# Queue order around xT, a later guard and later angle products in a gated-recurrence kernel with a cosine-gated feed-forward layer

## The chip, the core and the metric

The kernel runs on one core of one Trainium2 chip. The metric is the device time of one execution in microseconds (us). An engine takes its instructions strictly in the order of its own queue: TensorE (PE in the profile) multiplies, VectorE (DVE) and ScalarE (ACT) work elementwise, GpSimd (POOL) here does next to nothing but issue the DMAs of the guards, and SyncE (SP) issues all other DMAs. An instruction that waits holds up everything behind it in its queue.

## The reference

Two parts. The first is a linear recurrence with a complex decay for each of 4 batches and 8 heads, over 768 steps, with 48 x 48 states:

```python
mag = np.sqrt(a_re * a_re + a_im * a_im)
scale = np.minimum(mag, 0.999) / (mag + 1e-06)
a_re_n, a_im_n = (a_re * scale, a_im * scale)
for t in range(S):
    new_re = ar * S_re - ai * S_im      # ar, ai: the decay of step t
    new_im = ar * S_im + ai * S_re
    S_re, S_im = (new_re + kv, new_im)  # kv: k of step t times v of step t
    y[:, :, t] = np.einsum('bhd,bhde->bhe', q[:, :, t], S_re)
```

The second takes y, turned to x of 3072 tokens x 384, through a layer of width 2048:

```python
h = x @ w_in
g = h * np.cos(h)
return (g @ w_out).astype(np.float32)
```

## The kernel before

The sequence is cut into chunks of 128 steps. Two chunks make a group, so there are 12 groups, three to a batch. Within a chunk the recurrence becomes matrix products. Groups 0 and 1 and the conversion of the weights are written out by hand. After that, stage n of a loop (n = 2 to 11, lines 1730 to 1749) holds the work on several groups at once, and `weave` (line 1370) lays it out: each list of steps gets a stretch between 0 and 1, and the steps are traced in the order of their places. The order on each engine is then settled by a scheduler that goes through this trace with a clock of its own. A step that is earlier in the trace has priority, but a later one goes first where the earlier one isn't ready. `behind(a, b)` (line 543) fixes that a stands behind b in the queue that both use, without a wait. The order on PE is fixed by hand (`chain`).

What stage n holds, as far as it matters here:

- **Chunks of group n** (`chunks`, line 1417): the scores `sc` from kT and qT, the states `sp`, the outputs `yp`, which ACT copies to yT. Then `f_x` (line 1070) stores yT to DRAM as x, and `f_xt` (line 1079) loads it back turned, as xT. Then `ends` (line 844) sends one row of group n+1 out and back, and `load` fetches k, q and v of group n+2.
- **The first products of group n** (`first`, `mm1`, lines 1429 and 1230): `hp` from xT and w_in, at the end of the stage. ACT and DVE make the gates of them. In some of the eight, three short products take the place of one long one.
- **The second products of group n-1** (`seventh`, line 1314): seven products of quarters (Strassen's scheme) from gates and sums of gates. DVE forms those sums: `mixed` gives s1, `mixed_again` (line 1299) gives s3, then s2, then s4. In the trace an s2 mix reads `gate<-s,gate`. The third product reads the s2 mixes (`sum<-t_s,gate`). Results are stored from `ot` (lines 1350 and 1356).
- **The decay of group n+1**: `logs` (line 1409) runs `log_steps` (line 736), whose first step came at the end of the stage before. It ends in three products on DVE (lines 779, 785 and 788, the last of which reads im and writes tan) and a check of re on ACT (line 792). Then re and im of group n+2 are loaded into the same tiles, so these loads wait for the check and for the product with im. `prods` (line 1400) takes the sums over the steps (`lgs`), the arctangent of tan, the powers, and k and q times the powers. `phases` and `keys` (lines 1414 and 1383) go on with sine and cosine to `ks` and `qs`. DVE transposes these to `tr`, and `f_transpose` (line 945) sends tr out (`moved`) and loads kT in four pieces and qT in one. The next stage's scores read both.
- **A guard** (`guarded`, line 1443): GpSimd waits for a gate of group n-1, then loads 768 KB of raw weights into the buffer of tr, which ACT checks, and the same again. It waits for the gate tile with the highest number, 7. The order of the gates is 6, 7, 0, 1, 2, 3, 4, 5 in group 3 (4, 5, 0, 1, 2, 3, 6, 7 in group 2, plain from group 4 to 10).

k, q, re and im have one buffer each, and v has two. So k of group n+2 can be loaded once DVE has taken the product of k and the powers of group n+1.

Of the kernel before, what the change touches and what calls it, by code (L numbers as in the profile page):

```python
# [487 lines left out]
def fast_path(ctx, tc, q, k, v, a_re, a_im, moe_w_in, moe_w_out, out, least, odd, wide,  # L488
# [7 lines left out]
    nc = tc.nc  # L496
# [46 lines left out]
    def behind(ins, other):  # L543
        tc.add_manual_dep(ins.ins, other.ins.name, mybir.DependencyInfo(
            mybir.DependencyClass.NoSync, mybir.DependencyReason.DATA))
# [180 lines left out]
    def upper_half(g, x, scale):  # L726


        for name, tag in ("hi", "rs"), ("lo", "lo"):
            X[g][name] = gt.tile([C, G * DM], F32R, tag=tag, name=name)  # L730
        hi, lo = X[g]["hi"], X[g]["lo"]
        chain(nc.scalar.activation(out=hi, in_=x, func=AF.Copy, scale=scale))
        return lambda: vector.scalar_tensor_tensor(
            out=lo, in0=x, scalar=scale, in1=hi.bitcast(F32), op0=ALU.mult, op1=ALU.subtract)

    def log_steps(g, i, n):


        x = X[g]
        re, im = cut(x["re"], i, n), cut(x["im"], i, n)  # L740
        if i == 0:
            if g == 0:
                x["sin"] = temp("tan", 2)
            for name in "lg", "tan", "rs":
                x[name] = temp(name, 2 if name == "tan" else 1)
            both = gt.tile([C, 2, G * DM], F32, tag="pair", name="pair")
            x["Q"], x["mag"] = both[:, 0], both[:, 1]
        m2, sq, rs, mag = (cut(x[name], i, n) for name in ("lg", "tan", "rs", "mag"))
        for out_, in_ in (m2, re), (sq, im):
            if g == 0 and i > 0:  # L750
                if in_ is im:
                    yield
                vector.tensor_tensor(out=out_, in0=in_, in1=in_, op=ALU.mult)
            else:
                chain(nc.scalar.activation(out=out_, in_=in_, func=AF.Square))
        vector.tensor_tensor(out=m2, in0=m2, in1=sq, op=ALU.add)
        yield
        special(out=m2, in_=m2, func=AF.Ln, bias=tiny_b)
        special(out=mag, in_=m2, func=AF.Exp, scale=0.5)
        if g == 1:  # L760
            yield
        special(out=rs, in_=m2, func=AF.Exp, scale=-0.5)
        yield
        vector.scalar_tensor_tensor(out=mag, in0=re, scalar=0.0, in1=mag,
                                    op0=ALU.max, op1=ALU.add)
        vector.tensor_scalar(out=m2, in0=m2, scalar1=0.5, scalar2=math.log(CAP),
                             op0=ALU.mult, op1=ALU.min)
        yield
        special(out=rs, in_=rs, func=AF.Ln, scale=EPS, bias=one_b)
        special(out=sq, in_=mag, func=AF.Ln)  # L770
        special(out=sq, in_=sq, func=AF.Exp, scale=-1.0)
        yield
        vector.tensor_tensor(out=m2, in0=m2, in1=rs, op=ALU.subtract)
        yield

        lower = upper_half(g, m2, 1.0) if g >= PEG else None
        if lower and g > PEG:
            low = lower()
        product = vector.tensor_tensor(out=mag, in0=mag, in1=sq, op=ALU.mult)
        if lower and g > PEG:  # L780
            behind(product, low)
        elif lower:
            lower()
        yield
        vector.scalar_tensor_tensor(out=sq, in0=mag, scalar=2.0, in1=sq,
                                    op0=ALU.subtract, op1=ALU.mult)
        yield
        vector.scalar_tensor_tensor(out=sq, in0=sq, scalar=-1.0, in1=im,
                                    op0=ALU.mult, op1=ALU.mult)
        yield  # L790
        junk = stage["pool"].tile([C, DM], BF16, tag="below", name="below", bufs=1) if n == 1 else re
        checked = scalar.activation(out=junk, in_=re, func=AF.Relu, scale=-1.0,
                                    accum_out=odd[:, ds(next(odds), 1)])
        if g > PEG:
            behind(checked, tail["scalar"])

    def g_log(g, i, n):
        for _ in X[g].pop("steps", None) or log_steps(g, i, n):
            pass

    def summed_up(ps, g, i, name, ones):
# [497 lines left out]
    def mixed_again(g, p, name):  # L1299

        mix = X[g]["mix"][p]
        a, b = {"s3": ("s2", "s3"), "s2": ("s1", "s2"), "s4": ("s4", "s2")}[name]
        vector.tensor_tensor(out=mix[name], in0=mix[a], in1=mix[b], op=ALU.subtract)

    SEVEN = "a11", "a12", "a22", "s2", "s3", "s1", "s4"
    scale = 1.0 / (in_scale * out_scale)
# [7 lines left out]
    def seventh(g, p, part):  # L1314


        x, name = X[g], SEVEN[p]
        if p == 0 and part == 0:
            x["sum"] = pm.tile([C, E2], F32, tag="acc", name="sum", bufs=1)
            x["ot"] = [msb.tile([C, DM], F32, tag="ot", name="ot") for _ in range(G)]  # L1320

        alone = g == NG - 1 and p == 6
        summed = p in (0, 3, 5, 6) and not alone
        if not summed and part == 0:
            x["op"] = pm.tile([C, E2], F32, tag="m", name="op", bufs=2)
        ps = x["sum"] if summed else x["op"]
        for j in range(part * HJ // 2, (part + 1) * HJ // 2):
            matmul(ps, lhsT=left(g, name, j), rhs=right[name][:, j],
                   start=(j == 0 and (p == 0 or not summed)),
                   stop=(j == HJ - 1), skip_group_check=summed)  # L1330
        if part == 0:
            return
        c11, c12, c21, c22 = (x["ot"][i][:, ts(half, E2)] for i in range(2) for half in range(2))
        if g == NG - 1:
            c12 = rest
        if p in (0, 3, 5) or p == 6 and not alone:
            late["scalar"] = scalar.mul(out={0: c11, 3: c21, 5: c22, 6: c12}[p], in_=ps, mul=scale)
        if g == NG - 1 and p == 5:
            scalar.mul(out=c12, in_=ps, mul=scale)
        for part_ in {1: [c11], 2: [c21], 4: [c21, c22], 6: [c12] * alone}.get(p, []):  # L1340
            added = vector.scalar_tensor_tensor(out=part_, in0=ps, scalar=scale,
                                                in1=part_, op0=ALU.mult, op1=ALU.add)
            if alone:
                behind(added, late["read DVE"])
            late["vector"] = added
        row = g * G * C
        if g == NG - 1 and p == 1:
            behind(nc.sync.dma_start(out=out[ds(row, C), 0:E2], in_=c11), late["line"])
        elif p == 4:
            put = nc.sync.dma_start(out=out[ds(row + C, C), :], in_=x["ot"][1])  # L1350
            if g == NG - 1:
                behind(put, late["read SP"])
        elif p == 6 and alone:
            late["store"] = lambda: nc.scalar.dma_start(out=out[ds(row, C), E2:DM], in_=c12)
        elif p == 6:
            nc.sync.dma_start(out=out[ds(row, C), :], in_=x["ot"][0])

    def products(g, lo, hi):
        if g < PLAIN:
# [40 lines left out]
    def prods(g):  # L1400
        if not 0 <= g < NG:
            return
        if g not in (1, 2):
            yield from powers(g)
            yield lambda: g_angle(g, 0, G)
        yield lambda: (g_carry(g), g_split(g))
        yield lambda: (p_even(g, 0, G), p_apply(g, 0, G))

    def logs(g):
        yield from each(g_log, g)  # L1410
        if 0 <= g and g + 1 < NG:
            yield lambda: load(g + 1, ("re", "im"))

    def phases(g):
# [2 lines left out]
    def chunks(g):  # L1417
        for n in range(g * G, g * G + G):
            for hh in range(2):
                yield lambda n=n, hh=hh: f_scores(n, hh)  # L1420
            yield lambda n=n: f_state(n)
            yield lambda n=n: f_out(n)
        yield lambda: (f_x(g), f_xt(g))
        if PEG < g + 1 < NG:
            yield lambda: ends(g + 1)
        if g + 2 < NG:
            yield lambda: load(g + 2, ("k", "q", "v"))

    def first(g):
        late_ = [jp for jp in THREE if FROM[jp] == g + 1]  # L1430
# [8 lines left out]
    def wait_for(tile):  # L1439

        chain(nc.gpsimd.tensor_copy(out=after, in_=tile), "gpsimd")

    def guarded(g, count):

        if guards:
            yield lambda: wait_for(X[g]["gate"][NJ // 2 - 1][0:1, 0, 0:1])
        for _ in range(min(count, len(guards))):
            yield lambda: guard(guards.pop(0))

# [280 lines left out]
    for n in range(2, NG):  # L1730
# [4 lines left out]
        if FROM[THREE[0]] <= n < NG - 1:  # L1735
# [1 line left out]
        weave((mixes(n - 1, 2, 4), 0.0, 0.08), (logs(n + 1), 0.0, 0.02), (chunks(n), 0.0, 0.36),  # L1737
              (upper[2:] if plain else [], 0.0, 0.2), (products(n - 1, 0, 2 + (n < NG - 1)), 0.0, 0.365),
              (mixes_again(n - 1, "s3"), 0.06, 0.18), (mixes_again(n - 1, "s2"), 0.19, 0.27),
              (prods(n + 1), 0.2701, 0.2735), (second(n - 1, 1), 0.36, 0.5),  # L1740
              (mixes_again(n - 1, "s4"), 0.37, 0.48),
              (products(n - 1, 2 + (n < NG - 1), 7), 0.4, 0.56),
              (convert[0:1], 0.82, 0.82), (convert[1:2], 0.93, 0.93),
# [108 lines left out]
```

## Time and profile before

| | before |
|---|---|
| median of 3 runs | 653.19 us (650.83 to 653.82) |
| profiled execution | 651.08 us |
| its span, first to last instruction | 649.3 us |
| PE busy | 629.3 us (97%) |
| DVE busy | 522.2 us (80%) |
| ACT busy | 446.4 us (69%) |
| POOL busy | 30.8 us (5%) |
| granted TensorE clock | 0.999 |

A line of the timeline gives the start of a run of like instructions, its length, the engine, the line of the code, the operation, out<-in with shapes, and the count; in brackets stands the idle time ahead of it and what ended that. Line 691 is the helper through which nearly all matmuls go, line 680 that of most DVE and ACT instructions, line 711 that of ACT's table functions. SPq is the time that SyncE takes to issue a DMA, not the transfer. A line of the waits gives who waited for whom, the total in us, the number of waits and the longest. A line of the windows gives a stretch, its length, busy time of PE, PEld, DVE, ACT and POOL, the granted clock, the busy share of the DMA engines and what they moved in GB/s.

### The profile page before, as it was taken

The numbers are of one execution on the slowest core, as the hardware profiler recorded it, in microseconds if no ns is written. First come the engines' busy times: TensorE is split into PE (matmuls) and PEld (weight loads), VectorE is DVE, ScalarE is ACT, GpSimd is POOL, SyncE is SP. The second block draws the span as 40 slices with busy tenths as digits, with TensorE's granted clock in tenths as the row PEclk, the third lists the DMA queues.
The fourth block names the chain that finished last, engine by engine and source line by source line (L and its number), as shares of the span: only waits on it lengthen the run. The fifth ranks groups of instructions, "written<-read, shape, count | busy, mean of one in ns | idle before, by whom it ended". The sixth has DMA issues, their size and how long they took to land.

```text
span 649.3 us, 11364 instructions
## 1 busy us (share of the span) xinstructions
PE 629.3 (97%) x4279; PEld 571.5 (88%) x4279; DVE 522.2 (80%) x846; ACT 446.4 (69%) x803; POOL 30.8 (5%) x53
## 2 busy tenths in 40 slices
PE   8999999999998999999999999999999999999996
PEld 6888867777997889899999899899999899999996
DVE  6999989879789788798798888879878968964261
ACT  7898688284695697588588488589589479552340
POOL 4010200000000000000000000000000000000000
PEclk9999999999999999999999999999999999999999
DMA  9968755628538907927926935946945844351001
GB/s 240 246 184 207 223 167 124 171 49 225 116 89 189 258 2 175 224 91 177 249 63 143 248 97 123 245 98 162 235 94 144 232 87 124 132 111 49 24 1 32
DMA packets 232923, 94.94 MB, mean 146 GB/s; under 512 B 208701, under 2 KB 221246, under 8 KB 232858
## 3 DMA queue, kind: packets, MB, share of 16 engines
q1 hardware_dynamic: 225320, 68.51, 45.3%
q0 software_dynamic: 5824, 25.50, 12.1%
q8 instruction: 36, 0.59, 0.4%
q10 hardware_dynamic: 1714, 0.11, 0.2%
q14 instruction: 29, 0.24, 0.1%
HBM read 69.28 MB, written 24.81 MB: 145 GB/s over the span
## 4 chain that ended last, share of the span: by engine, by line
PE 69%; ACT 10%; DVE 8%; DMA 7%; issue 3%; SPq 1%; ACTq 0%; DVEq 0%
PE hp L691 29%; PE op L691 13%; PE sum L691 8%; PE sc L691 5%; PE yp L691 4%; DMA xT<-x 4%; PE sp L691 3%; PE hb L691 3%; DMA im<-in_a_im_dram 2%; DVE pair L680 2%; ACT tan L711 1%; DVE tan L680 1%; ACT rs L711 1%; PE phs L691 1%; SPq L584 1%
## 5 line engine op out<-in xcount | busy, mean ns | idle before, releaser
L691 PE MATMUL hp<-xT,w_in 128*128 128x256 f32 (+1 forms) x768 | 165.6, 373 | 5.9 <-DMA xT<-x 5.2
L691 PEld LDWEIGHTS hp<-xT,w_in 128*128 128x128 f32 x768 | 141.5, 190 | 27.2 <-DVE qs L680 4.4
L711 ACT ACTIVATE gate<-hp,half_pi_b 128x512 f32<-128x512 f32 x96 | 65.9, 687 | 72.1 <-PE hp L691 56.0
L691 PE MATMUL op<-w_out,gate 128*128 128x192 f32 (+1 forms) x464 | 102.7, 371 | 0.0
L691 PEld LDWEIGHTS op<-w_out,gate 128*128 128x128 f32 x464 | 78.7, 190 | 15.2 <-issue 0.4
L680 DVE TENSOR_TENSOR gate<-hp,gate 128x512 f32<-128x512 f32 x62 | 42.4, 686 | 30.7 <-ACT junk L680 30.3
L680 ACT ACTIVATE junk<-hp 128x512 bf16<-128x512 f32 x96 | 56.7, 590 | 0.0
L691 PE MATMUL sum<-w_out,gate 128*128 128x192 f32 x304 | 54.9, 328 | 0.4 <-DVE gate L680 0.4
L691 PE MATMUL sc<-qT,kT 96*128 96x128 f32 x384 | 51.0, 278 | 2.1 <-issue 1.8
L691 PEld LDWEIGHTS sc<-qT,kT 96*128 96x128 f32 x384 | 47.2, 191 | 5.1 <-issue 2.7
L691 PEld LDWEIGHTS sum<-w_out,gate 128*128 128x128 f32 x304 | 49.3, 190 | 0.8 <-DVE gate L680 0.7
L680 DVE SCALAR_TENSOR_TENSOR gate<-hp,gate 128x512 f32<-128x512 f32 x34 | 23.5, 691 | 22.8 <-ACT junk L680 22.8
L691 PE MATMUL hp<-xh,wh 128*128 128x256 f32 x204 | 36.9, 290 | 0.0
L680 DVE TENSOR_TENSOR atm<-sc,causal 128x512 f32<-128x512 f32 x48 | 32.5, 685 | 5.2 <-PE sc L691 5.0
L691 PE MATMUL hp<-xl,wl 128*128 128x256 f32 x204 | 35.2, 281 | 0.0
L680 ACT COPY yT<-yp 48x512 f32<-48x512 f32 x44 | 25.4, 578 | 13.8 <-PE yp L691 13.1
L680 DVE TENSOR_TENSOR gate<-gate 128x256 f32<-128x256 f32 x80 | 31.7, 418 | 3.1 <-PE op L691 2.5
L691 PE MATMUL yp<-atm,v 128*48 128x128 f32 x352 | 33.5, 277 | 0.0
L680 ACT ACTIVATE ot<-sum 128x192 f32<-128x192 f32 x39 | 12.5, 321 | 29.3 <-PE sum L691 29.3
L707 ACT ACT_TABLE_LOAD x24 | 30.8, 1283 | 1.2 <-PEq L1836 0.7
L691 PE MATMUL sum<-t_s,gate 128*128 128x192 f32 x160 | 29.4, 330 | 1.6 <-DVE gate L680 1.6
L691 PEld LDWEIGHTS hp<-xh,wh 128*128 128x128 f32 x204 | 29.8, 189 | 0.5
(163 smaller groups left out, 1246.2 us busy)
## 6 DMA issues: line engine op xcount, KB each, us to landing
moved<-tr SPq DMA_DIRECT2D x20, 768.0 KB
raw<-in_moe_w_in_dram POOLq DMA_DIRECT2D x16, 768.0 KB, 5.9
raw<-in_moe_w_out_dram POOLq DMA_DIRECT2D x16, 768.0 KB, 5.0
kT<-moved SPq DMA_DIRECT2D x40, 192.0 KB
qT<-moved SPq DMA_DIRECT2D x10, 768.0 KB
k<-in_k_dram SPq DMA_DIRECT2D x24, 192.0 KB
q<-in_q_dram SPq DMA_DIRECT2D x24, 192.0 KB
v<-in_v_dram SPq DMA_DIRECT2D x24, 192.0 KB
```

Source lines behind the costliest of these rows:

```text
L584: put(out=tile_[lo:hi, i_], in_=steps[lo + by:hi + by, i_])
L680: ins = getattr(self.engine, op)(**kw)
L691: chain(nc.tensor.matmul(out, **kw), "tensor")
L707: chain(nc.scalar.preload_act_table_set(table))
L711: chain(nc.scalar.activation(func=func, **kw))
```

## The change

Four edits:

1. `load` of k, q and v of group n+2 goes through `back_first`, which puts each of these DMAs behind the last DMA of xT in SyncE's queue. The two stores of `ot` are put behind it too.
2. The guard waits for the gate that is last in the order of its group.
3. `log_steps` yields "angles" ahead of the three products, for groups above 2. `g_log` stops there, and a new step `angles`, at 0.2695 to 0.2699 of the stage, goes on. The first of the three products is put behind the last s2 mix (`late["mixed"]`). The check of re on ACT is put behind what ACT's chain held last at the split of the logarithm (`late["upper"]`).
4. The loads of re and im of group n+2 move with the products, from the end of `logs` (by 0.02 of the stage) to the end of `angles`.

```diff
         lower = upper_half(g, m2, 1.0) if g >= PEG else None
+        late["upper"] = tail["scalar"]
         if lower and g > PEG:
-            low = lower()
+            lower()
+            yield "angles"
         product = vector.tensor_tensor(out=mag, in0=mag, in1=sq, op=ALU.mult)
-        if lower and g > PEG:
-            behind(product, low)
-        elif lower:
+        if "mixed" in late:
+            behind(product, late["mixed"])
+        if lower and g == PEG:
             lower()
...
         if g > PEG:
-            behind(checked, tail["scalar"])
+            behind(checked, late["upper"])
 
     def g_log(g, i, n):
-        for _ in X[g].pop("steps", None) or log_steps(g, i, n):
+        x = X[g]
+        x["steps"] = x.get("steps") or log_steps(g, i, n)
+        for at in x["steps"]:
+            if at == "angles":
+                return
+
+    def g_rest(g):
+        for _ in X[g]["steps"] if g > PEG else []:
             pass
...
-        vector.tensor_tensor(out=mix[name], in0=mix[a], in1=mix[b], op=ALU.subtract)
+        late["mixed"] = vector.tensor_tensor(out=mix[name], in0=mix[a], in1=mix[b], op=ALU.subtract)
...
             put = nc.sync.dma_start(out=out[ds(row + C, C), :], in_=x["ot"][1])
-            if g == NG - 1:
-                behind(put, late["read SP"])
+            behind(put, late["read SP"] if g == NG - 1 else late["x"])
...
         elif p == 6:
-            nc.sync.dma_start(out=out[ds(row, C), :], in_=x["ot"][0])
+            behind(nc.sync.dma_start(out=out[ds(row, C), :], in_=x["ot"][0]), late["x"])
...
     def logs(g):
         yield from each(g_log, g)
-        if 0 <= g and g + 1 < NG:
+
+    def angles(g):
+        if g < NG:
+            yield lambda: g_rest(g)
+        if g + 1 < NG:
             yield lambda: load(g + 1, ("re", "im"))
...
         if g + 2 < NG:
-            yield lambda: load(g + 2, ("k", "q", "v"))
+            yield lambda: load(g + 2, ("k", "q", "v"), put=back_first)
+
+    def back_first(**kw):
+        put = nc.sync.dma_start(**kw)
+        behind(put, late["x"])
+        return put
...
         if guards:
-            yield lambda: wait_for(X[g]["gate"][NJ // 2 - 1][0:1, 0, 0:1])
+            yield lambda: wait_for(X[g]["gate"][X[g]["order"][-1]][0:1, 0, 0:1])
...
-              (prods(n + 1), 0.2701, 0.2735), (second(n - 1, 1), 0.36, 0.5),
+              (angles(n + 1), 0.2695, 0.2699), (prods(n + 1), 0.2701, 0.2735), (second(n - 1, 1), 0.36, 0.5),
```

## The prediction

> **What bounds the kernel now.** I read the page first, then the waits of TensorE, then the timelines of PE, SP, DVE, ACT and POOL in stages 3 to 10, and last the chain of waits and windows of half a us.
>
> ```profile
> span 649.3 us, 11364 instructions
> ...
> PE 629.3 (97%) x4279; PEld 571.5 (88%) x4279; DVE 522.2 (80%) x846; ACT 446.4 (69%) x803; POOL 30.8 (5%) x53
> ```
>
> PE is busy for 97% of the span, so no faster engine can bring much: all that can be won is PE's idle time, some 20 us with the start and the tail. The profiled execution took 651.08 us, 2.11 below the median of 653.19 and inside the runs (650.83 to 653.82). I work the sum out against it and subtract the result from the median.
>
> ```profile
> PE hp L691 <- DMA xT<-x: 5.2, 5, 1.8
> PE sum L691 <- DVE gate L680: 2.0, 5, 0.5
> ```
>
> These two waits, 5.2 and 2.0 us, are idle time of PE that repeats in the loop. The timeline of PE shows where they fall, and a third one:
>
> ```profile
> 206.59 15.81 PE L691 MATMUL hp<-xT,w_in 128*128 128x256 f32 x72 [1.84 <-DMA xT<-x]
> ...
> 228.47 1.13 PE L691 MATMUL sc<-qT,kT 96*128 96x128 f32 x8 [1.81 <-issue]
> ...
> 260.52 1.75 PE L691 MATMUL hp<-xT,w_in 128*128 128x256 f32 x7 [0.54 <-DMA xT<-x]
> ...
> 279.58 1.13 PE L691 MATMUL sc<-qT,kT 96*128 96x128 f32 x8
> ...
> 359.84 10.60 PE L691 MATMUL hp<-xT,w_in 128*128 128x256 f32 x48 [1.34 <-DMA xT<-x]
> ...
> 378.83 1.06 PE L691 MATMUL sc<-qT,kT 96*128 96x128 f32 x8
> ...
> 396.46 2.22 PE L691 MATMUL sum<-t_s,gate 128*128 128x192 f32 x12 [0.37 <-DVE gate L680]
> ...
> 410.44 1.75 PE L691 MATMUL hp<-xT,w_in 128*128 128x256 f32 x7 [0.31 <-DMA xT<-x]
> ...
> 429.43 1.05 PE L691 MATMUL sc<-qT,kT 96*128 96x128 f32 x8
> ...
> 509.56 10.60 PE L691 MATMUL hp<-xT,w_in 128*128 128x256 f32 x48 [1.16 <-DMA xT<-x]
> ...
> 528.55 1.06 PE L691 MATMUL sc<-qT,kT 96*128 96x128 f32 x8
> ```
>
> The brackets at 206.59, 260.52, 359.84, 410.44 and 509.56 are the five waits of the first products for xT: 1.84, 0.54, 1.34, 0.31 and 1.16 in stages 3, 4, 6, 7 and 9. At 396.46 stands one of five waits for an s2 mix, 0.37; their mean is 2.0 / 5 = 0.4, and stages 4, 6, 7 and 9 have one each. At 228.47 the scores of stage 4 wait 1.81 us, put down to "issue". The other rows of scores show no idle time ahead; I use them below.
>
> **Edit 1, k, q, v and the stores behind xT.** SP's queue and DVE's in stage 7:
>
> ```profile
> 396.85 2.46 SPq L584 DMA_DIRECT2D im<-in_a_im_dram  x4
> 399.42 2.16 SPq L1075 DMA_DIRECT2D x<-yT  x2
> 405.01 1.02 SPq L584 DMA_DIRECT2D k<-in_k_dram  x2
> 406.14 0.67 SPq L1084 DMA_DIRECT2D xT<-x  x1
> ...
> 412.06 1.49 SPq L1350 DMA_DIRECT2D out_dram<-ot  x1
> ```
>
> ```profile
> 395.12 0.94 DVE L680 SCALAR_TENSOR_TENSOR tan<-tan,im 128x768 f32<-128x768 f32 x1
> 395.99 1.09 DVE L680 TENSOR_TENSOR gate<-s,gate 128x256 f32<-128x256 f32 x3
> ...
> 404.03 0.95 DVE L680 TENSOR_TENSOR pair<-k,pair 128x768 f32<-128x768 f32 x1
> ```
>
> The k load is issued at 405.01, when DVE's product of k and the power ends (404.03 + 0.95 = 404.98). xT stands right behind it and goes out at 406.14, though its own condition, that x has landed, can be met earlier. How much earlier, and what it costs to run with k's packets ahead:
>
> ```profile
> 299.94 1.72 SPq L1075 DMA_DIRECT2D x<-yT  x2
> ...
> 305.29 0.37 SPq L1084 DMA_DIRECT2D xT<-x  x1
> ...
> 550.67 0.38 SPq L1084 DMA_DIRECT2D xT<-x  x1
> ```
>
> ```profile
> 406.14 4.16 DMA xT<-x
> ```
>
> ```profile
> 553.00:553.50 0.50, 0.50 (x4) 0.50 (x4) 0.50 (x2) 0.31 (x1) 0.00 (x0) 1.00 0.48 164
> 553.50:554.00 0.50, 0.50 (x5) 0.50 (x4) 0.50 (x2) 0.48 (x2) 0.00 (x0) 1.00 0.00 0
> ```
>
> In stage 5 x is issued until 301.66 and xT goes out at 305.29, with SP idle just before, so x takes at most 3.6 us to land. In stage 7 it would be there at 401.58 + 3.6 = 405.2, 0.9 before 406.14. Behind k's 2 x 192 KB xT takes 4.16 us. In stage 10, where no k is loaded, it is issued at 550.67, and the traffic ends in the slice from 553.0 (0.48 busy, then none): about 2.8 us, and I take 3.0 with the signal. So xT should land at 408.2, 2.1 earlier than at 410.3, and that is more than any of the five waits. Bounds of this edit: nothing, up to 5.2. The stores stand behind xT already (412.06 after 406.14); that part removes nothing, and adds at most a wait that is met. What is queued behind the later k, q and v is the row of the decays and `moved`, which is the question further down.
>
> **Edit 3, the products behind the s2 mixes.** Nothing is added. In stage 7 three of the s2 mixes (1.09 us) run after the product with im. Put ahead of it, they end some 3 us earlier, as three products of 0.95 no longer stand before them, and the wait of 0.4 goes. The product with im then ends at 396.06 + 1.09 = 397.15. Its first reader is the arctangent:
>
> ```profile
> 398.75 0.84 ACT L711 ACTIVATE tan<-tan 128x768 f32<-128x768 f32 x1
> ```
>
> ACT gets to it at 398.75, after its exponentials and a table load, so 1.6 us of cover remain; without that cover each us would go into the keys. The im load waits for the same product and is later by 1.09; its next reader, the first step of a logarithm, stands behind the first products, which start 13 us after 396.85 (410.44). But x is issued behind im (399.42 after 396.85 + 2.46), so x may be up to 1.09 later too. Taken off the 2.1 this leaves 1.0, enough for stages 4 and 7, about enough for 9, and 0.3 short in stage 6 and 0.8 in stage 3. If the scheduler instead sends x out before im, which is now late, xT has over 3 us to spare. Either fits the result, as the next bound is elsewhere. The check of re keeps its length and its place behind the split.
>
> **Edit 4** moves ten DMA issues per stage with these products, and has no cost of its own.
>
> **Edit 2, the guard.** Kept for last, because it shows that next bound:
>
> ```profile
> 216.25 0.74 POOL L631 DMA_DIRECT2D raw<-in_moe_w_in_dram  x1 [0.58 <-ACT junk L680]
> ```
>
> ```profile
> 215.69 6.53 SPq L960 DMA_DIRECT2D kT<-moved  x4
> 222.33 0.78 SPq L962 DMA_DIRECT2D qT<-moved  x1
> ...
> 273.20 0.80 SPq L962 DMA_DIRECT2D qT<-moved  x1
> ...
> 367.05 3.91 SPq L960 DMA_DIRECT2D kT<-moved  x4
> 371.06 1.09 SPq L962 DMA_DIRECT2D qT<-moved  x1
> ...
> 422.02 1.22 SPq L962 DMA_DIRECT2D qT<-moved  x1
> ...
> 521.74 0.64 SPq L962 DMA_DIRECT2D qT<-moved  x1
> ...
> 566.96 5.15 SPq L960 DMA_DIRECT2D kT<-moved  x4
> ```
>
> In group 3 gate 7 is the second of eight. So the guard's 768 KB start at 216.25, in the middle of the four kT loads, whose issue then takes 6.53 us against 3.91 in stage 6. qT follows at 222.33, and the scores wait for it: 228.47 - 222.33 = 6.14 us. With the gate that is last, the load starts after the first products, and qT goes out about 2.6 earlier. The bounds are nothing (kT is slow for another reason) and both idle times of that stage, 1.81 + 1.84 = 3.65. I take 2.6. In all other groups gate 7 is last anyway.
>
> [...]
>
> **What is late next.** The same rows say how early the scores could start. Stage 5's follow qT's issue by 279.58 - 273.20 = 6.38 without a wait, so 6.14 to 6.38 is the landing, and I take 6.25. The room of the others, each for the first products ahead of it: stage 5 0.1; stage 7 378.83 - 371.06 - 6.25 = 1.5; stage 8 429.43 - 422.02 - 6.25 = 1.15; stage 10 528.55 - 521.74 - 6.25 = 0.55. qT depends on DVE's transposes, hence on the arctangent and on the scores of the stage before, and not on xT. So time won at xT or at the s2 mixes comes back as a wait for qT as soon as it exceeds the room.
>
> | stage | idle that goes | room | gain |
> |---|---|---|---|
> | 3 | 1.84 + 1.81 | 2.6 from the guard | 2.6 |
> | 4 | 0.54 + 0.4 | 0.1 | 0.1 |
> | 6 | 1.34 + 0.4 | 1.5 | 1.5 |
> | 7 | 0.31 + 0.4 | 1.15 | 0.7 |
> | 9 | 1.16 + 0.4 | 0.55 | 0.55 |
>
> The sum is 5.45: 651.08 becomes 645.6, and the median 653.19 - 5.45 = 647.7.
>
> **The rivals.**
>
> - *qT is no floor.* k, q and v are out sooner where xT is, `moved` starts on emptier DMA engines and qT lands earlier by what is needed. Then all idle time goes: 5.2 + 2.0 + 1.8 = 9.0, 644.2. Against it: qT's chain starts at the arctangent, which doesn't move.
> - *The bytes are only put off.* k, q and v, 1.15 MB, lie closer to `moved`, kT and qT on the same DMA engines, and qT lands later by the 1.1 us for which k stood ahead of xT. The rooms shrink by 1.1: stage 3 gives 1.5, 4 loses 1.0, 6 gives 0.4, 7 nothing, 9 loses 0.55. That is 0.35, so 652.8: no change. [...] Against it: in the last stage, with no k, q or v loaded, the issue of kT still takes 5.15 us (566.96), no less than with them.
> - *Slower.* The scheduler keeps the s2 mixes where they are and only the products go back. The last mix ends at 395.99 + 1.09 = 397.08, the three products at 397.08 + 3 x 0.95 = 399.9, and im, with x behind it, is late by 399.9 - 396.06 = 3.9. xT has 2.1 of that; the other 1.8 falls on the five stages with waits, 9.0, and the guard gives 2.6 back: 653.19 + 6.4 = 659.6. It decides from a delay of 2.1 + 2.6 / 5 = 2.6 on. Against it: no mix has anything else to wait for, and each has priority over the products in the new trace.
> - *It doesn't do what it says.* The orders are a scheduler's; the stores were behind xT before, and a changed trace may put something else there, such as the check of re between the exponentials (0.9 late in each arctangent, inside the cover). Then the guard alone is left: 653.19 - 2.6 = 650.6, or nothing.
>
> **How the numbers follow.** A measurement of this kernel can tell about 0.5%, 3.3 us, from no change. My forecast has 0.55, qT as no floor 0.13, the bytes put off 0.14, slower 0.08, and the change without its effect 0.10. Faster by more than 0.5% are the first two, less a little for a forecast whose guard term fails (2.85 left): 0.66. Slower by more than that is 0.08 and half of 0.02 for delays between; I say 0.09. The rest, 0.25, is the same. The range goes from the largest gain, 644.2, less 1.2 for runs as low as the profiled one, to the case of the bytes put off, a little short of it: 643.0 to 652.0. What lies outside is the slower case and part of the unchanged ones, about 0.15 to 0.2.
>
> **What would show it.** Right: in SP's timeline xT before k, and from it no idle time ahead of `hp`; no wait of `sum` for `gate`; the guard's load of stage 4 after its scores have begun, instead of at 216.25; kT's issue near 216 taking about 4 us; and small idle times ahead of the first scores of stages 5, 7 and 10, where now there are none. Wrong: the scores of those stages without idle time (then the gain is larger), x issued later than the end of `yp` by more than today with a wait for xT left (the slower case), or an arctangent later against the scores than 398.75 - 378.83 = 19.9 us.

## The result and the profile after

| | before | after |
|---|---|---|
| median | 653.51 us (650.83 to 654.52, 4 runs) | 670.61 us (669.76 to 671.38, 4 runs) |
| profiled execution | 651.08 us | 671.38 us |
| its span | 649.3 us | 669.6 us |
| granted clock | 0.999 | 0.984 |

The ratio is 1.0268, with a 95% interval of 1.0234 to 1.0302: slower, where the prediction said faster. By the medians that is 17.1 us; the two profiled executions differ by 20.3, as the one before, 651.08, lies near the fastest of its runs. The page's first lines, and the waits of TensorE after:

```profile
span 669.6 us, 11345 instructions
...
PE 632.7 (94%) x4279; PEld 574.6 (86%) x4279; DVE 522.5 (78%) x846; ACT 446.7 (67%) x803; POOL 29.8 (4%) x53
```

```profile
PE hp L691 <- DMA xT<-x: 20.5, 2, 10.6
PE yp L691 <- DVE atm L680: 2.0, 5, 0.9
PE sc L691 <- DMA qT<-moved: 1.6, 2, 0.8
PE sc L691 <- issue: 1.5, 1, 1.5
...
PE sum L691 <- DVE gate L680: 0.4, 1, 0.4
```

VectorE, ScalarE and GpSimd are as busy as before, within 1 us; PE is busy for 3.4 us more, at a lower clock (below). The five short waits for xT and the s2 waits are gone, as forecast (the 0.4 left stands in the tail, and stood there before: the prediction counted it among its five s2 waits). But two waits for xT have come that were not there, 20.5 us together; the span is longer by 669.6 - 649.3 = 20.3. The timeline of PE shows them in stages 2 and 3:

```profile
150.38 2.74 PE L691 MATMUL op<-w_out,gate 128*128 128x384 f32 x8
163.71 22.57 PE L691 MATMUL hp<-xT,w_in 128*128 128x256 f32 x96 [10.59 <-DMA xT<-x]
186.11 1.06 PE L691 MATMUL sc<-qT,kT 96*128 96x128 f32 x8
...
226.44 18.43 PE L691 MATMUL hp<-xT,w_in 128*128 128x256 f32 x72 [9.94 <-DMA xT<-x]
248.99 1.06 PE L691 MATMUL sc<-qT,kT 96*128 96x128 f32 x8
```

Before, the row of the first of these scores was:

```profile
174.36 1.06 PE L691 MATMUL sc<-qT,kT 96*128 96x128 f32 x8
```

The scores of stage 3 (the row of `sc` behind the first products of stage 2) start at 186.11 instead of 174.36, 11.75 late, and those of stage 4 at 248.99 instead of 228.47, another 8.77. From there to the end of the span it is 669.6 - 248.99 = 420.6 after and 649.3 - 228.47 = 420.8 before: nothing more is lost, and nothing gained. Why xT is late stands in SyncE's timeline of the same two stages, with VectorE's beside it:

```profile
145.04 1.69 SPq L1084 DMA_DIRECT2D x<-yT  x2
153.67 0.36 SPq L1269 DMA_DIRECT2D out_dram<-ot  x1
158.46 0.34 SPq L966 DMA_DIRECT2D moved<-tr  x1
158.97 0.37 SPq L1093 DMA_DIRECT2D xT<-x  x1
...
208.79 0.82 SPq L1084 DMA_DIRECT2D x<-yT  x2
221.08 0.34 SPq L966 DMA_DIRECT2D moved<-tr  x1
221.53 0.38 SPq L1093 DMA_DIRECT2D xT<-x  x1
...
423.47 0.39 SPq L1093 DMA_DIRECT2D xT<-x  x1
...
424.85 1.02 SPq L1442 DMA_DIRECT2D k<-in_k_dram  x2
```

```profile
156.25 2.19 DVE L680 STREAM_TRANSPOSE tr<-ks 128x1536 f32<-128x1536 f32 x1
...
218.87 2.19 DVE L680 STREAM_TRANSPOSE tr<-ks 128x1536 f32<-128x1536 f32 x1
```

Between x and xT stands `moved`, the transfer of the next group's keys. It waits for VectorE's transpose, which ends at 156.25 + 2.19 = 158.44 and 218.87 + 2.19 = 221.06, and it is issued 0.02 us later each time. xT, whose data had long landed (x is issued by 146.73 and 209.61, and the DMA share is 0.00 from 152.5 to 154.5 and from 215.5 to 221.5), goes out right behind it. In stage 2 a plain store stands there as well, until 153.67. From stage 4 on the queue is as intended: in stage 7 xT goes out at 423.47, and k behind it at 424.85.

### The profile page after: what moved, and what is told of

Read it like the earlier page. It is cut to its first block, busy times and chain, and to the rows that moved or that the text cites. A ratio compares the mean times of both kernels' runs of the same rounds, so it can differ in the third digit from the quotient of the medians.

```text
span 669.6 us, 11345 instructions
## 1 busy us (share of the span) xinstructions
PE 632.7 (94%) x4279; PEld 574.6 (86%) x4279; DVE 522.5 (78%) x846; ACT 446.7 (67%) x803; POOL 29.8 (4%) x53
## 4 chain that ended last, share of the span: by engine, by line
PE 65%; DVE 12%; ACT 11%; DMA 7%; issue 4%; SPq 1%; ACTq 0%; DVEq 0%
PE hp L691 23%; PE op L691 15%; PE sum L691 10%; PE sc L691 5%; PE yp L691 5%; PE sp L691 3%; DVE gate L680 2%; DMA qT<-moved 2%; DMA xT<-x 2%; ACT gate L711 2%; ACT junk L680 2%; DVE hp L680 1%; PE hb L691 1%; DVE pair L680 1%; PE phs L691 1%
## 5 line engine op out<-in xcount | busy, mean ns | idle before, releaser
L691 PE MATMUL hp<-xT,w_in 128*128 128x256 f32 (+1 forms) x768 | 170.1, 381 | 21.3 <-DMA xT<-x 20.5
L691 PEld LDWEIGHTS hp<-xT,w_in 128*128 128x128 f32 x768 | 144.5, 194 | 43.7 <-DMA xT<-x 21.4
L691 PE MATMUL sp<-v,ks 128*96 128x48 f32 x320 | 29.7, 246 | 0.0
```

The lines of the kernel that those rows point to most:

```text
L691: chain(nc.tensor.matmul(out, **kw), "tensor")
```

## Theories

**Q, the head of the queue.** Edit 1 pins k, q, v and the stores behind xT, but `moved` is pinned to nothing. With what stood around xT gone, the scheduler put `moved` ahead of xT in stages 2 and 3, and SyncE's queue stood still for its wait. **A rival, the angle edit:** im, and x behind it, go out later, and the products of VectorE stand elsewhere. **Another, the bytes:** k, q and v meet `moved`, kT and qT on the DMA engines. Q says that a pin that restores the order gives the forecast's time; the rivals say that it doesn't.

## The experiments

Each ratio is to the kernel before on the same chip (medians 649.69, 650.01 and 650.56 us in the three groups: e1 to e4, e5 to e8, e9 to e12). `late["x"]` is the last DMA of xT.

**The order mended.** The changed kernel, with `moved` and the last plain store behind xT:

```diff
-        nc.sync.dma_start(out=moved.rearrange("q (r b) x j -> (q r) b x j", b=NB), in_=tr)
+        behind(nc.sync.dma_start(out=moved.rearrange("q (r b) x j -> (q r) b x j", b=NB), in_=tr), late["x"])
...
+            if g == 1 and i:
+                behind(put, late["x"])
```

> The changed kernel with two more NoSync edges: the transposed keys and queries (moved) and the last plain store of group 1 stand behind xT in SyncE's queue. Theory Q (queue): in stages 2 and 3 xT stands behind the keys' moved in the queue and waits for DVE's transpose; both idle times of 10.6 and 9.9 us go, with the slow clock after them, and the time comes to 646 to 651 us. Rival A (angles): x or im is late because the angle products are late, and xT would wait anyway: the idle times stay, 665 us or more. Rival C (contention): x lands late, since its bytes share the DMA engines: the idle times shrink by less than half, about 660 us.

Measured: 645.37 us, ratio 0.9936 (0.9914 to 0.9958); and again in the third group:

> The same kernel as in the first of these runs (the changed kernel with the keys' transfer and the last plain store behind x), as the standard of the runs beside it on this chip. Expected at the ratio that it had: 0.9914 to 0.9958, 644 to 647 us. The interval decides what the guard and the angle edit are worth in the runs below.

Measured: 645.46 us, 0.9923 (0.9897 to 0.9950). The span of the profiled execution is 642.8 us. Its SyncE in stage 3, its PE in stages 2 and 3, and its waits:

```profile
196.68 0.82 SPq L1084 DMA_DIRECT2D x<-yT  x2
200.00 0.38 SPq L1093 DMA_DIRECT2D xT<-x  x1
...
208.88 2.46 SPq L966 DMA_DIRECT2D moved<-tr  x2
213.88 3.69 SPq L969 DMA_DIRECT2D kT<-moved  x4
```

```profile
153.11 7.93 PE L691 MATMUL hp<-xT,w_in 128*128 128x256 f32 x36
161.72 13.22 PE L691 MATMUL hp<-xT,w_in 128*128 128x256 f32 x60 [0.67 <-DVE gate L680]
174.77 1.06 PE L691 MATMUL sc<-qT,kT 96*128 96x128 f32 x8
...
204.37 16.04 PE L691 MATMUL hp<-xT,w_in 128*128 128x256 f32 x72
224.52 1.06 PE L691 MATMUL sc<-qT,kT 96*128 96x128 f32 x8
```

```profile
PE yp L691 <- DVE atm L680: 2.6, 5, 0.9
...
PE sc L691 <- issue: 1.0, 1, 1.0
```

No wait for xT is left. Two pins turn 1.0268 into 0.9936 and 0.9923, some 22 us. So neither the bytes nor the angle edit made the changed kernel slow: both are in here, unchanged.

**One swap in the kernel before.** The converse: one pin is added there, which puts xT behind `moved` in stage 2 (with it, q, v and a plain store also go out ahead of xT).

```diff
+    SWAP = 3
...
+        put = nc.sync.dma_start(out=moved.rearrange("q (r b) x j -> (q r) b x j", b=NB), in_=tr)
+        if g == SWAP and name == "kT":
+            behind(late["x"], put)
```

> The kernel before with one edge: in stage 2 alone, SyncE's queue gets xT of the next group behind the keys' transfer of that same group, which waits for VectorE's transpose. Nothing else is edited. The queue theory expects the projections of stage 2 to wait about 10 us for xT (the transpose of the keys ended 5 us after x went out in the changed kernel, and xT lands 3 us after its issue), TensorE's clock at 0.5 to 0.7 for some microseconds after it, and the whole time 9 to 13 us above the kernel before. A theory that puts the loss down to the amount of transfers or to VectorE's work expects less than 3 us, since nothing is added.

Measured: 664.05 us in one run, 14 above the median before; the span is 662.3, 13.0 above. Its waits and its SyncE:

```profile
PE hp L692 <- DMA xT<-x: 13.6, 4, 10.4
```

```profile
158.68 0.34 SPq L958 DMA_DIRECT2D moved<-tr  x1
159.07 0.43 SPq L1087 DMA_DIRECT2D xT<-x  x1
```

The longest wait is 10.4, as expected; the whole is a little above the 9 to 13 expected by the median and at their upper end by the span, and a stretch of slow clock comes with the wait (0.50 from 163.7 to 169.0). xT goes out at 159.07, as soon as `moved` is issued (158.68 + 0.34); the store ahead of both was out by 154.24, so it is `moved` that holds it. With this swap alone the loss of stage 2 is there without any of the four edits. Q is shown from both sides.

**The keys' transfer alone.** As e1, without the pin of the store.

> The changed kernel with one edge more, not two: the keys' transfer stands behind x, but in stage 2 the last plain store may still stand ahead of xT. In the changed kernel that store was issued at 153.67, and the transfer of the keys at 158.46. So xT goes out near 154 and the projections of stage 2 wait some 4 to 6 us for it instead of 10.6, with a stretch of slow clock behind it; stage 3 has no such wait. Time 648 to 652 us, ratio 0.998 to 1.002 (the whole fix minus a wait of 4 to 6 us). If the store did no harm, the ratio is that of the standard beside it.

Measured: 653.24 us, 1.0031 (1.0010 to 1.0051), a little above what was expected. Its SyncE and PE in stage 2:

```profile
157.23 0.36 SPq L1269 DMA_DIRECT2D out_dram<-ot  x1
157.76 0.38 SPq L1093 DMA_DIRECT2D xT<-x  x1
```

```profile
161.31 23.67 PE L691 MATMUL hp<-xT,w_in 128*128 128x256 f32 x96 [4.64 <-DMA xT<-x]
```

The plain store alone holds xT for a wait of 4.64, and the first products behind it take 23.67 us instead of 7.93 + 13.22 = 21.15: 7.2 us. Against e9 the run is 653.24 - 645.46 = 7.8 slower. (This profiled execution, 657.34 us, is the slowest of its runs; it also comes into stage 2 some 3.4 us late, by a second wait for xT, 6.7 - 4.6 = 2.1 us by its waits, and slow products behind it, seven in 2.64 us at 89.75; e9 has no such wait, and eleven of these products in 2.54 us at 89.73.)

**Without the load edit.** The changed kernel with k, q and v loaded as before.

```diff
-            yield lambda: load(g + 2, ("k", "q", "v"), put=back_first)
+            yield lambda: load(g + 2, ("k", "q", "v"))
```

> The changed kernel with k, q and v of two groups ahead loaded as before; the stores, the guard and the angle products stay changed. Theory Q: it was the load edit that let the scheduler put moved ahead of xT; without it no idle time of 10 us, 648 to 652 us, with waits for xT of about 1 us as before. Rival A: the angle products are the cause, 665 us or more.

Measured: 650.06 us, 1.0019 (0.9986 to 1.0052). Its waits:

```profile
PE hp L691 <- DMA xT<-x: 9.5, 6, 2.2
```

No long wait, though the short ones have grown, to 2.2 us where about 1 was expected. Without edit 1's loads the scheduler keeps `moved` behind xT, with the other edits all there. So it is the load edit that opens the place; whether it does so alone, in the kernel before, was not run. Why the scheduler's clock then takes `moved` there in stages 2 and 3 and not in the others was not shown.

**The guard alone, the angles alone** (edit 2, and edits 3 and 4, each in the kernel before):

> The kernel before with the guard's edit alone. By the prediction's step kT's issue in stage 3 shortens from 6.5 to about 4 us and the scores of stage 4 come 1.8 to 2.6 us earlier: 650.5 to 651.5 us against 653.3. Rival: kT's issue there is slow for another reason; no change, and a wait of 1.8 us stays.

> The kernel before with the angle products and the loads of re and im moved (edits 3 and 4) and nothing else. By the prediction's step the five waits for an s2 mix (2.0 us) go, and what the keys leave room for stays won: 0.5 to 1.5 us faster. Rival: the masks of the scores now stand behind the mixes, yp waits for them (2.0 us in the changed kernel), and it comes out the same to 1 us slower.

Measured: 649.38 us, 0.9992 (0.9969 to 1.0015), and 650.43 us, 1.0020 (0.9998 to 1.0042). Neither alone moves the time clear of no change: the guard's 1.8 to 2.6 us and the angles' 0.5 to 1.5 were not seen. In e3 the wait ahead of the scores of stage 4 is gone, yet they start at 228.44, as before (228.47). What was won went into the products ahead of them, 17.49 us for 15.81, part of it at half clock (below):

```profile
206.83 17.49 PE L691 MATMUL hp<-xT,w_in 128*128 128x256 f32 x72 [1.95 <-DMA xT<-x]
```

```profile
PE hp L691 <- DMA xT<-x: 4.3, 5, 2.0
PE sum L691 <- DVE gate L680: 3.2, 5, 1.7
```

The waits for xT fell from 5.2 to 4.3 us and those of `sum` for gates went from 2.0 to 3.2, by one of 1.66 in stage 4; e8 has the same one with the guard untouched, so it is not shown to be the guard's. In e4 the s2 waits are gone, and the waits for xT went from 5.2 to 7.5:

```profile
PE hp L691 <- DMA xT<-x: 7.5, 6, 1.9
```

The 1.81 us ahead of the scores of stage 4 is gone in e4 too (they start at 226.55 without a wait), although the guard's load still starts early there, at 215.49. So that wait has not the guard alone for its cause. (This profiled execution of e4, 647.33 us, is the fastest of its runs.)

**One edit left out of the right order.** Without the guard edit (twice):

> The changed kernel with the guard at its old tile, and with the keys' transfer and the last plain store behind x. What the guard is worth once xT is ahead: the forecast has 2.6 us (the wait of the scores of stage 4 for qT comes back, 1.8 us in the kernel before), so 648 us, ratio 0.997. If the guard is worth nothing, as the run with the guard alone says by its median (ratio 0.9992), the ratio is that of the same kernel with the guard, 0.9936, to 0.002. Between the two, 0.995, leaves it undecided.

> The right order with the guard at its old tile, which gave a ratio of 0.9958 (0.9934 to 0.9983), now on one chip with the standard. The forecast's 2.6 us for the guard expects it 2 to 3 us above the standard (ratio between the two medians 1.003 to 1.005); a guard worth nothing expects them within 0.6 us.

Measured: 647.94 us, 0.9958 (0.9934 to 0.9983), and 649.44 us, 1.0000 (0.9975 to 1.0025). Against e9, on the same chip as the second, that is 649.44 - 645.46 = 4.0 slower; by the first ratio against e1's it is 0.9958 - 0.9936, or 1.4 us, and in the profiled executions 645.7 - 642.8 = 2.9. Stage 3 itself, from its first scores to those of stage 4, takes 51.69 us in e7 and 51.45 in e12, against 49.75 in e9: 1.94 and 1.70 of it. The kT issue there is short in both, 3.89 and 3.76 us with the guard at its old tile; it is qT's issue behind it that takes 4.03 and 3.58, against 1.12 in e9. Without the angle edit:

> The changed kernel without its angle edit (angle products and the loads of im and x where the kernel before has them), with the keys' transfer and the last plain store behind x. The queue theory (what was lost is xT waiting behind the keys' transfer) expects xT ahead of the keys' transfer in every stage, no wait of the projections for xT above 0.5 us and a time of 645 to 649 us, ratio 0.990 to 0.998; the waits of the sums for the gate (2.0 us in the kernel before) stay or grow to 3 us. The rival that the angle edit itself made the changed kernel slow expects this run to be faster than the same kernel with the angle edit (ratio 0.9936) by 2 us and more: 643 us or less.

Measured: 675.40 us, 1.0397 (1.0353 to 1.0440). Not as expected: xT is in its place, and yet this is the slowest of all. Its waits and VectorE's timeline in stage 6:

```profile
PE yp L691 <- DVE atm L680: 19.9, 12, 3.4
```

```profile
338.60 0.96 DVE L680 SCALAR_TENSOR_TENSOR pair<-re,pair 128x768 f32<-128x768 f32 x1 [0.54 <-ACT pair L711]
339.48 0.55 DVE L680 TENSOR_SCALAR lg<-lg 128x768 f32<-128x768 f32 x1
339.95 0.68 DVE L680 TENSOR_TENSOR atm<-sc,causal 128x512 f32<-128x512 f32 x1
```

The same thing in another queue: the second mask of the scores (`atm`), which `yp` needs, stands behind steps of the next group's logarithm that wait for ScalarE. So this run tells of an order, not of the angle edit. The rival, which expected it faster than e1, is answered by e1 itself and by the next run, which comes out slower than e9. That one holds those steps behind the masks:

```diff
+        for at, held in ((1, "held0"), (1, "held1"), (1, "held2"), (3, "held3")):
+            if g >= PEG and i * 2 + hh == at and g + 1 < NG and held in X[g + 1]:
+                behind(X[g + 1][held], y["masked"])
```

(`held0` to `held3` are the minimum, the maximum, the subtraction and the product of magnitudes.)

> The kernel without the angle edit that took 675 us, with VectorE's order of the kernel before for the masks: in each stage the maximum, the minimum and the subtraction of the next group's logs stand behind the second mask, and the product of magnitudes behind the fourth. Theory of the head of the queue (in that run the masks stood behind operations that waited for ScalarE, so the output products waited 19.9 us): those waits fall under 4 us and the time falls by 22 us and more, to 646 to 652 us. Against the same order with the angle edit (the standard beside it) it should then be 0 to 3 us slower, the worth of the angle edit by the forecast's waits of the sums (2.0 us). If the loss had another source (the loads of im and x at their old place), it stays above 660 us.

Measured: 649.79 us, 0.9997 (0.9969 to 1.0025). The 25 us are back, so it was the masks' place. `yp` still waits 5.6 us, not under 4, and against e9 it is 4.3 slower, not 0 to 3; how much of that is the masks and how much the s2 mixes stays open.

**The masks first.** The right order, with the product of magnitudes behind the last mask traced ahead of it:

```diff
         if "mixed" in late:
             behind(product, late["mixed"])
+            behind(product, late["masked"])
```

> The changed kernel with the keys' transfer and the last plain store behind x in SyncE's queue, and with one more edge: VectorE's product of magnitudes stands behind the last mask of its stage, where in the run before it stood ahead of the second chunk's masks. In that run the output products waited for VectorE's masks 6 times, 3.2 us in all. If those waits are what kept the right order from giving more, they go, and the time is 1 to 3 us below that run's 645.4 (ratio to the kernel before 0.989 to 0.992). If the time that they held only moves to the next late thing (the queries' transfer, the sums), the ratio stays at 0.992 to 0.995. The waits for the masks must be gone from the profile either way.

Measured: 644.24 us, 0.9911 (0.9880 to 0.9942). The waits for the masks fell to 1.1 us, but are not gone. From the scores of stage 3 to those of stage 11 it is 574.87 - 176.54 = 398.3 us, in e9 572.95 - 174.77 = 398.2: what was saved there came back elsewhere. The lowest median of all, but its interval overlaps e1's and e9's, so it is not shown to be better.

## Why the prediction was wrong

- **The step that failed** is edit 1's: "Bounds of this edit: nothing, up to 5.2." A loss was left out without a reason. The text had the two halves of it: "What is queued behind the later k, q and v is the row of the decays and `moved`", taken as staying behind, and in the fourth rival "The orders are a scheduler's ... and a changed trace may put something else there". But that rival was priced as a gain left out, with the check of re as its example. Its price as a loss was in the rows of before: `moved` can't go out before the transpose, and in SyncE's timeline of before it goes out at 158.26 in stage 2, 9 us behind xT at 149.23. Two swaps cost 20.5 us here, one 13. The two rows of before:

```profile
149.23 0.37 SPq L1084 DMA_DIRECT2D xT<-x  x1
...
158.26 2.47 SPq L957 DMA_DIRECT2D moved<-tr  x2
```

- **The other pins** failed in the same way. "The stores stand behind xT already ... adds at most a wait that is met" holds for the two stores that the diff pins. A third, the plain store, is not pinned, and it cost 7 to 8 us in stage 2 (e11).
- **For the order that was meant the sum came out near, in part by luck.** Forecast 5.45 us, or 0.83% of 653.19; e1 and e9 gave 0.64% (0.42 to 0.86) and 0.77% (0.50 to 1.03). By stage, in e9's profile against before's: stage 3 4.36 for 2.6, stage 4 0.03 for 0.1, stage 6 1.27 for 1.5, stage 7 0.70 for 0.7, stage 9 1.05 for 0.55. Stages 8 and 10 lose 0.94 and 1.00, which was not foreseen, and that about cancels what stage 3 gave too much. In stage 3 qT was no floor: it goes out 42.9 us after the stage's first scores (217.69 - 174.77), against 48.0 before (222.33 - 174.36), 5 us earlier and not 2.6. Stage 8's loss has the size of two new waits for masks (0.22 and 0.87). In e5 these fell to 0.22 and 0.34 and the stage loses 0.63, but stage 10 loses 1.75 there; why is not shown.
- **The guard as a price of its own** (2.6, "the guard alone is left") failed: alone it gives 0.5 us (a loss of 1.0 to a gain of 2.0). In the right order it is worth 1.4 to 4.0. The others are alike: left out, the load edit costs 1.0019 - 0.9936, some 5 us (e2, without the two pins), and the angle edit 4.3 (e10, with its waits for masks), each about all of the gain, and the two tried alone give none. The prices hang together. In e4 what is won at the s2 mixes comes back in waits for xT (stage 4: 0.50 gone, 1.58 for 0.54; stage 7: 0.37 gone, 1.10 for 0.31), and the wait that the prediction put down to the guard goes without the guard's edit. The prediction saw this for qT only, and called it room.
- **The bytes put off:** qT is waited for by 0.3 us in e9, and by 1.0 more under "issue". That rival's 5 us of lost gain didn't come. **Slower by late products** didn't either: the s2 mixes did go ahead.
- **Of the signs:** xT before k, no s2 wait and the guard's load behind the scores of stage 4 (255.94, behind 248.99) were seen. Of the small idle times named, ahead of the scores of stages 5, 7 and 10, only that of stage 5 came (1.48 after, 1.01 in e9); the others stood at stages 9 and 11. kT's issue in stage 3 took 3.69 in e9, against 6.53. One sign of being wrong came, without harm seen: the arctangent of stage 7 starts 20.3 us behind the scores, against 19.9. The sign for a swap, something other than k ahead of xT in SyncE's queue, was not on the list.

## What to carry to other kernels

When an edit moves or pins one entry of an in-order queue, write down every entry that may then stand ahead of the one that matters, and when each of these can go at the earliest; its wait is the price, and it is a loss. Where the order is a scheduler's, pin what must not go ahead, and not only what one wants moved. Waits that follow one another on the same engine need not have separate prices: here one wait went by either of two edits, and time won at one wait came back at the next. Price such edits together, and don't expect one of them alone to give its share.

## What the runs showed of the hardware

After its two long waits, of 10.59 and 9.94 us, TensorE didn't come back at full speed. The windows after, in stages 2 and 3 (the third column from the right is the granted clock):

```profile
163.70:167.00 3.30, 3.29 (x8) 2.67 (x9) 0.17 (x1) 0.00 (x0) 0.00 (x0) 0.51 0.82 115
167.00:170.00 3.00, 3.00 (x16) 2.64 (x15) 0.70 (x3) 1.26 (x3) 0.00 (x0) 1.00 1.20 231
...
226.40:229.00 2.60, 2.56 (x6) 2.11 (x7) 0.56 (x1) 0.00 (x0) 0.00 (x0) 0.50 0.88 112
229.00:232.00 3.00, 3.00 (x9) 2.35 (x9) 0.34 (x2) 0.03 (x1) 0.00 (x0) 0.53 1.18 237
232.00:235.00 3.00, 3.00 (x15) 2.65 (x14) 1.56 (x2) 2.40 (x5) 0.00 (x0) 1.00 1.04 238
```

The clock is about 0.5 for the first 3.3 and 5.6 us of the products. It costs 22.57 - 21.15 = 1.4 and 18.43 - 16.04 = 2.4 us on top of the waits (against e9's rows). After the 4.64 us of e11 it is the same (0.50 and 0.54 from 161.3 to 167.0; 23.67 against 21.15), and after the 10.44 us of e8 it is 0.50 until 169.0. In windows of half a us of the run after, the clock falls within the waits themselves: it is 1.00 up to 156.5, 3.4 us into the first, and 0.50 from 157.0; in the second it is 1.00 up to 221.5, 5.0 us in, and 0.50 from 222.0. What sets the time until it falls and the time until it is back was not shown. It was also seen low behind a shorter wait: in e3 the clock falls after a wait of 1.95 us, some 1.5 us into the products that start at 206.83:

```profile
206.80:207.50 0.70, 0.67 (x3) 0.62 (x4) 0.70 (x2) 0.00 (x0) 0.00 (x0) 1.00 0.91 182
...
208.50:209.00 0.50, 0.50 (x2) 0.35 (x2) 0.50 (x1) 0.00 (x0) 0.00 (x0) 0.50 0.79 96
...
211.00:211.50 0.50, 0.50 (x2) 0.41 (x2) 0.50 (x2) 0.50 (x1) 0.00 (x0) 0.50 1.18 452
```

In e2 waits of 2.09 and 2.21 us at the same place of the stage, one stage apart, leave it at 1.00. In e8 the same products take 17.49 us as in e3, behind a wait of 2.04 us. So a wait near 2 us was followed by half clock in e3 and not in e2, and the price was 1.7 us (17.49 us, in e8 too, for products that take 15.81 before); what decides it was not shown.
